# A pooled attention and feed-forward kernel: the fifth tile's scores move into the first run, the first batch's main keys times v become one float32 product, and two later steps move

## The chip, the cores and the metric

The kernel runs on one core of a Trainium2 chip. The metric is the device time of the whole program in microseconds (us), the median of several runs.

TensorE (PE) multiplies, with its weight loads shown apart as PEld. VectorE (DVE), ScalarE (ACT) and GpSimd (POOL) do the elementwise work, and SyncE (SP) issues most of the DMAs. All of them have queues of their own and meet at semaphores.

## The reference

```python
# q, k, v: (8, 8, 576, 64): batch, heads, tokens, head size
k_p = k.reshape(B, H, 72, 8, D).mean(axis=3)
v_p = v.reshape(B, H, 72, 8, D).mean(axis=3)
scores = scale * q @ k_p.T;  scores -= scores.max(-1)
attn = exp(scores);  attn = attn / (attn.sum(-1) + 1e-9)
x = (attn @ v_p) as tokens x 512          # 4608 x 512
h = x @ w_in                              # 512 -> 2048
out = maximum(0.01 * h, h) @ w_out        # 2048 -> 512
```

Everything is float32. Each head has 72 pooled keys; the kernel treats 64 of them as main keys and the last 8 as a remainder.

## The kernel before

The feed-forward part has most of the work. Its products are made of float32r parts: a value is split into a high part (a cast) and a low part (the value less the high part), and three products stand for one (high by high, high by low, low by high). The weights are split in the same way on the chip, by steps that `convert` makes: two ScalarE instructions (L209, L210) and three VectorE instructions (L211, L212, L215) in the first step, a ScalarE cast (L219) and a VectorE subtraction (L220) in the second.

The tokens lie in nine chunks of 512. The first two batches' first 512 tokens are chunks 0 and 1, their last 64 tokens each go into `x_tail`, and the others follow. `runs` lists the passes over the feature tiles: the first run takes chunk 0 with feature tiles 0 to 7, the next two runs take halves of chunk 1 with the same tiles, the fourth and fifth runs take the other eight tiles for chunks 1 and 0, and from the sixth run on a chunk has all sixteen. The seventh run is the fourth chunk (index 3). The last chunks are done with sums of weight blocks, formed earlier by `prepare` (L1192 on VectorE with casts L1195 and subtractions L1199), put into DRAM by POOL's DMA queue (`put_away`, L1179) and read back in the last runs.

In a run, a feature tile has a first product `m1` (ph, L1143 to L1145, twelve instructions), a leaky ReLU and a split (L1148, L1151 on ScalarE, L1152 on VectorE), and two tiles later a second product `m2` (acc, L1361 to L1363). `ph` has two banks. Each half of `m1` and of `m2` is a beat. Attention steps are set between the beats: step i of a run's list goes out when its share of the beats is reached. In the first run that list starts with `TAIL_STEPS`, and the second batch follows.

The steps of a batch are written as names with a tile and a group of four heads: `q` transposes a tile of queries, `sa` makes scores and their exponentials (pss L600, reduction L608, e L610), `sb` divides by the sums (L621, L622 on VectorE, `at` L624 and L628 on POOL), `pu` transposes the attention (pp L701) and splits it (pT, L703, L706, L710), `au` multiplies it with v (pa, L725 to L728, four products for each pair of heads) and splits the result into x (L744, L745). `ku` and `vu` put pooled k and v in place: for v that is `v_hi` (L513), `v_lo` (L516) and the remainder (L522 to L531). `FIRST` is the order of the first batch's steps, in which `c` is a step of the weights; all of it stands ahead of the first run.

TensorE's order is as written (`manual_schedule`). The orders of VectorE, ScalarE, POOL and SP are made by a list scheduler when the program is built: among instructions that it takes to be ready, the one written earlier goes first, and an instruction that is ready runs ahead of its place in the text if its engine is free. From the last runs on POOL and SP are as written, too.

Outputs go from the accumulator into tiles `o` (three buffers), the left half by ScalarE (L1400) and the right half by VectorE (L1401), and then by a DMA to `out`.

```python
PLAN = {REST + 1: (2, 10, 36), REST + 2: (3, 3, 34), REST + 3: (1, 3, 20), REST + 4: (2, 3, 34)}
...
    forming, formed = (sums_in(n), 0) if n in PLAN else (None, 0)
    many, begin, until = PLAN.get(n, (0, 0, 1))
...
    while forming and formed < min(1, (beat - begin) / (until - begin)) * STEPS_OF * many:
```

`REST` is 4, so the entry `REST + 2` is the seventh run: three pairs of weight sums, in seven steps each, from beat 3 until beat 34.

Of the kernel before, what the change touches and what calls it, by code (L numbers as in the profile page):

```python
# [10 lines left out]
F32 = mybir.dt.float32  # L11
F32R = mybir.dt.float32r
# [12 lines left out]
def tile_pooled_attention_ffn(  # L25
# [9 lines left out]
    nc = tc.nc  # L35
# [32 lines left out]
    )  # L68
    TAIL_STEPS = "pu40 au20 pu41 au21"
# [77 lines left out]
    }  # L147

# [17 lines left out]
    def spare(f, i, shape, dtype, name):  # L166

        return wts.tile(shape, dtype, tag=f"w{i}_{f}", name=name)
# [272 lines left out]
    def pin(ins):  # L441
        return tc.keep_in_program_order(ins) if pinned else ins
# [57 lines left out]
    def place_v(b, sums, rem):  # L500
# [10 lines left out]
        for i in range(2):  # L511
            r = slice(64 * i, 64 * i + 64)
            pin(nc.scalar.mul(v_hi[r, :, i, :], sums[r], 1.0 / POOL))  # L513
        for i in range(2):
            r = slice(64 * i, 64 * i + 64)
            pin(nc.vector.scalar_tensor_tensor(  # L516
                v_lo[r, :, i, :], sums[r], 1.0 / POOL, v_hi[r, :, i, :].bitcast(F32),
                op0=ALU.mult, op1=ALU.subtract,
            ))
# [166 lines left out]
    def piece_tiles(b, j, g):  # L686
        if b > 0 or g == 0 or j == 2:
            return pT
        return {
            part: spare(10 - n // 2, n % 2, t.shape, F32R, f"pT_{part}{b}_{j}_{g}")  # L690
            for n, (part, t) in enumerate(pT.items())
        }

    def p_unit(b, t, g, at, pc, o):
# [8 lines left out]
        ins = nc.scalar.copy(pc["hi"][:, :, o : o + n], pp[:, 0:3, :n])  # L703
        if b == 0:
            anchor["act"] = ins
        nc.vector.tensor_tensor(  # L706
            pc["lo"][:, :, o : o + n], pp[:, 0:2, :n], pc["hi"][:, 0:2, o : o + n].bitcast(F32),
            op=ALU.subtract,
        )
# [4 lines left out]
    def av_unit(b, j, g, pc):  # L714
# [3 lines left out]
        for i in range(2):  # L718
# [6 lines left out]
            nc.tensor.matmul(pa, vh, pc["hi"][:, i, :w], start=True, stop=False)  # L725
            nc.tensor.matmul(pa, vh, pc["lo"][:, i, :w], start=False, stop=False)  # L726
            nc.tensor.matmul(pa, vl, pc["hi"][:, i, :w], start=False, stop=False)  # L727
# [760 lines left out]
    for n, pieces in enumerate(beside):  # L1488
# [15 lines left out]
        if n == REST:  # L1504

            us.insert(2, lambda: None)
            units[-1] = [lambda: None] * AHEAD + us[:AHEAD]
            us = us[AHEAD:]
# [12 lines left out]
    PLAN = {REST + 1: (2, 10, 36), REST + 2: (3, 3, 34), REST + 3: (1, 3, 20), REST + 4: (2, 3, 34)}  # L1521
# [152 lines left out]
```

## Time and profile before

| | us |
|---|---|
| median of 3 runs | 916.62 |
| lowest and highest | 916.54 to 917.75 |
| the profiled execution's own time | 916.26 |
| its span | 914.4 |

The span lies from the first to the last recorded instruction; 1.86 us of the profiled execution's time lie around it. In the rows, a time is in us from the start of the span, "x4" is a number of instructions, and a bracket at the end of a row gives how long the engine stood idle ahead of it and what released it. Every float32 product, such as L600, is recorded as two instructions, and a float32r product as one. The engines work in a pipeline, so the length of an instruction is longer than the step to the next one; where a rate is meant, it is the difference of two starts. The clock is a share of full speed: 1.00 is 2.4 GHz and 0.50 is 1.2 GHz.

### The profile page before, as it was taken

Reading aid. Unit: us, or ns where it says so; the run is one execution under the profiler, and the core shown is the slowest. Engines: PE = TensorE matmul, PEld = TensorE weight load, DVE = VectorE, ACT = ScalarE, POOL = GpSimd, SP = SyncE. Lnnn points to the kernel's source line nnn. Section 1 sums busy time; section 2 is a strip of 40 time slices with the busy share of each in tenths; the row PEclk is TensorE's granted clock in tenths of the full one; section 3 lists DMA queues with packets and bytes.
Section 4 is the critical chain, followed back from the end, with each engine's and each line's share of the span. In section 5 each row is a group of like instructions: output and inputs, shape, how many; then the busy total and the mean of one; then the engine's idle time right before and its main releaser. Section 6 shows DMA issues by size and latency. Waiting matters only on the chain.

```text
span 914.4 us, 14169 instructions
## 1 busy us (share of the span) xinstructions
PE 886.6 (97%) x4731; PEld 764.5 (84%) x4731; DVE 520.4 (57%) x1229; ACT 446.2 (49%) x1397; POOL 257.6 (28%) x458
## 2 busy tenths in 40 slices
PE   5689999999999999999999999999999999999998
PEld 4568889887888888888888888888999999999997
DVE  6999569546377654874456437655665643342222
ACT  5798559345244533543454336353654553353322
POOL 4511110342527432552243134624320230010000
PEclk9799999999999999999999999999999999999999
DMA  9965231327356542644254317630875254425332
GB/s 268 315 205 168 63 76 47 84 64 198 98 162 155 137 89 73 184 124 106 51 144 116 103 31 195 162 104 1 204 211 144 67 153 141 124 77 161 104 112 74
DMA packets 151321, 116.53 MB, mean 127 GB/s; under 512 B 100689, under 2 KB 127825, under 8 KB 151249
## 3 DMA queue, kind: packets, MB, share of 16 engines
q1 hardware_dynamic: 136272, 82.47, 34.2%
q10 hardware_dynamic: 11904, 24.78, 9.3%
q0 software_dynamic: 3072, 8.39, 2.6%
q8 instruction: 37, 0.61, 0.3%
q14 instruction: 36, 0.29, 0.1%
HBM read 85.07 MB, written 30.54 MB: 126 GB/s over the span
## 4 chain that ended last, share of the span: by engine, by line
PE 84%; DVE 4%; DMA 3%; ACT 2%; POOL 2%; SPq 1%; issue 1%; POOLq 0%; DVEq 0%; ACTq 0%
PE acc L1361 13%; PE acc L1362 13%; PE acc L1363 13%; PE ph L1143 8%; PE ph L1145 8%; PE ph L1144 8%; PE ends_y L1268 7%; PE ends_x L1268 6%; PE pss L600 3%; PE pa L726 1%; PE pa L728 1%; PE pa L727 1%; PE pa L725 1%; DMA v1raw<-in_v_dram 1%; DVE x_tail L1192 1%
## 5 line engine op out<-in xcount | busy, mean ns | idle before, releaser
L1361 PE MATMUL acc<-w,gh 128*128 128x512 f32 x576 | 227.9, 396 | 1.2 <-DVE o L1401 1.2
L1362 PE MATMUL acc<-w,gh 128*128 128x512 f32 x576 | 225.4, 391 | 0.0
L1363 PE MATMUL acc<-w,gl 128*128 128x512 f32 x576 | 224.6, 390 | 0.0
L1143 PE MATMUL ph<-xh,w 128*128 128x512 f32 (+1 forms) x416 | 159.2, 383 | 1.6 <-DVE gl L1152 1.6
L1144 PE MATMUL ph<-xl,w 128*128 128x512 f32 (+1 forms) x416 | 155.9, 375 | 0.0
L1145 PE MATMUL ph<-xh,w 128*128 128x512 f32 (+1 forms) x416 | 155.9, 375 | 0.0
L1363 PEld LDWEIGHTS acc<-w,gl 128*128 128x128 f32 x576 | 108.1, 188 | 23.9 <-DVE gl L1152 0.5
L1361 PEld LDWEIGHTS acc<-w,gh 128*128 128x128 f32 x576 | 108.6, 188 | 21.0 <-DVE o L1401 1.7
L1362 PEld LDWEIGHTS acc<-w,gh 128*128 128x128 f32 x576 | 108.5, 188 | 18.0
L610 ACT ACTIVATE e<-pss,red 128x72 f32<-128x72 f32 (+1 forms) x320 | 97.6, 329 | 43.6 <-DVE red L608 43.4
L1148 ACT ACTIVATE ph<-ph 128x512 f32<-128x512 f32 (+1 forms) x104 | 58.0, 558 | 87.9 <-PE ph L1145 87.4
L1152 DVE TENSOR_TENSOR gl<-ph,gh 128x512 fp32r<-128x512 f32 (+1 forms) x104 | 66.6, 641 | 54.3 <-ACT gh L1151 53.8
L1143 PEld LDWEIGHTS ph<-xh,w 128*128 128x128 f32 x416 | 78.7, 189 | 15.3 <-DVE gl L1152 2.1
L1145 PEld LDWEIGHTS ph<-xh,w 128*128 128x128 f32 x416 | 78.6, 189 | 14.2
L1144 PEld LDWEIGHTS ph<-xl,w 128*128 128x128 f32 x416 | 78.8, 189 | 12.9
L644 POOL TENSOR_TENSOR at<-e,red 128x128 f32<-128x128 f32 (+1 forms) x120 | 50.6, 442 | 129.6 <-DVE red L641 74.8
L610 ACT ACTIVATION_READ_ACCUMULATOR e<-pss,red 128x1 f32 (+1 forms) x320 | 68.8, 215 | 0.0
L681 DVE STREAM_TRANSPOSE pp<-blocks 128x384 f32<-128x384 f32 (+1 forms) x60 | 44.5, 760 | 39.7 <-DMA blocks<-rows 39.5
L608 DVE TENSOR_REDUCE red<-pss 128x4 f32<-128x288 f32 (+1 forms) x80 | 35.8, 452 | 52.4 <-PE pss L600 51.1
L703 ACT CAST pT_hi<-pp 128x384 fp32r<-128x384 f32 (+1 forms) x80 | 36.9, 479 | 49.7 <-DVE pp L681 46.0
L1151 ACT CAST gh<-ph 128x512 fp32r<-128x512 f32 (+1 forms) x104 | 57.9, 556 | 2.5
L600 PEld LDWEIGHTS pss<-kT,qT 128*128 128x128 f32 x320 | 47.0, 199 | 6.4 <-ACT qT L577 1.5
(293 smaller groups left out, 1529.1 us busy)
## 6 DMA issues: line engine op xcount, KB each, us to landing
seat<-kept ACTq DMA_DIRECT2D x31, 512.0 KB
rows<-at SPq DMA_DIRECT2D x48, 192.0 KB
blocks<-rows SPq DMA_DIRECT2D x48, 192.0 KB
out_dram<-o SPq DMA_DIRECT2D x34, 256.0 KB
w_bits<-in_moe_w_in_dram SPq DMA_DIRECT2D x16, 512.0 KB
w_bits<-in_moe_w_out_dram SPq DMA_DIRECT2D x16, 512.0 KB
q<-in_q_dram SPq DMA_DIRECT2D x96, 64.0 KB
w<-kept ACTq DMA_DIRECT2D x21, 256.0 KB
```

What stands on the lines that cost most here:

```text
L600: nc.tensor.matmul(sc[:, 2 * SP * i : 2 * SP * (i + 1)], qT[:, p, :], kT[:, p, :, :].rearrange("d i s -> d (i s)"), start=True, stop=True,)
L610: ins = nc.scalar.activation(e[:n, h, :], scv[:n, h, :], AF.Exp, bias=mx[:n, h : h + 1], accum_out=sm[:n, h : h + 1],)
L1143: nc.tensor.matmul(ph, w[:, 0, ks], xh[kk][:, r], start=kk == 0, stop=False)
L1144: nc.tensor.matmul(ph, w[:, 0, ks], xl[kk][:, r], start=False, stop=False)
L1145: nc.tensor.matmul(ph, w[:, 1, ks], xh[kk][:, r], start=False, stop=kk == NK - 1)
L1148: nc.scalar.activation(ph, ph, AF.Prelu, alpha=0.01)
L1151: casts.append(nc.scalar.copy(gh, ph))
L1152: lows.append(nc.vector.tensor_tensor(gl, ph, gh.bitcast(F32), op=ALU.subtract))
L1268: nc.tensor.matmul(out, w[:, stay, ks], move, start=start and i + n == 0, stop=i + n == 3, skip_group_check=True,)
L1361: nc.tensor.matmul(a, gh[:, r], hi, start=first, stop=False)
L1362: nc.tensor.matmul(a, gh[:, r], lo, start=False, stop=False)
L1363: nc.tensor.matmul(a, gl[:, r], hi, start=False, stop=last)
```

## The change

The scores of the first batch's fifth tile (`sa40 sa41 sb40 sb41`) leave `FIRST` and become the first four steps of the first run's list. For the first batch, the product of the 64 main keys with v is a single float32 product of whole values (`v_whole`, `whole`), where there were three float32r products; so the low parts of attention and of v are not formed, and the ScalarE copy of the transposed attention becomes two, one for the remainder and one for the main keys. The remainder's product stays. The third batch's `vu` (index 2, `att[VIA]`) is written some steps later, behind `sb11`. The weight sums of the fourth chunk's run are formed from beat 8 until 37. `v_whole` lies in the buffer that later holds a part of the second chunk's x, and so do the `whole` tiles.

```diff
--- before.py
+++ after.py
@@ -64,9 +64,9 @@
     FIRST = (
         "lk ku q0 q1 sa00 sb00 sa01 sb01 lv sa10 sb10 sa11 sb11 q2 sa20 sa21 vu pu00 pu10 c c q3 "
         "pu01 pu11 c sb20 sb21 au00 sa30 sa31 c au01 c pu20 pu21 sb30 sb31 c c pu30 pu31 c au10 au11 "
-        "c q4 c c / sa40 sa41 sb40 sb41 c c c"
+        "c q4 c c / c c c"
     )
-    TAIL_STEPS = "pu40 au20 pu41 au21"
+    TAIL_STEPS = "sa40 sa41 sb40 sb41 pu40 au20 pu41 au21"
     VIA = 2
     SPLIT = 8
     HALF = CH // 2
@@ -145,6 +145,9 @@
         "hi": const.tile([P, 3, PMAX], F32R, name="pT_hi"),
         "lo": const.tile([P, 2, PMAX], F32R, name="pT_lo"),
     }
+
+    v_whole = one.tile([P, NK, 2, D], F32, tag="xl1_1", name="v_whole")
+    nc.gpsimd.memset(v_whole, 0.0)
 
     tiny = const.tile([P, 4], F32, name="tiny")
     nc.gpsimd.memset(tiny, 1e-9)
@@ -510,8 +513,11 @@
             sums = pvm.rearrange("a (p d) -> a p d", p=NK)
         for i in range(2):
             r = slice(64 * i, 64 * i + 64)
-            pin(nc.scalar.mul(v_hi[r, :, i, :], sums[r], 1.0 / POOL))
-        for i in range(2):
+            if b == 0:
+                nc.scalar.mul(v_whole[r, :, i, :], sums[r], 1.0 / POOL)
+            else:
+                pin(nc.scalar.mul(v_hi[r, :, i, :], sums[r], 1.0 / POOL))
+        for i in range(2 if b else 0):
             r = slice(64 * i, 64 * i + 64)
             pin(nc.vector.scalar_tensor_tensor(
                 v_lo[r, :, i, :], sums[r], 1.0 / POOL, v_hi[r, :, i, :].bitcast(F32),
@@ -684,12 +690,13 @@
         return pp
 
     def piece_tiles(b, j, g):
-        if b > 0 or g == 0 or j == 2:
+        if b > 0:
             return pT
-        return {
-            part: spare(10 - n // 2, n % 2, t.shape, F32R, f"pT_{part}{b}_{j}_{g}")
-            for n, (part, t) in enumerate(pT.items())
-        }
+        hi = pT["hi"]
+        if g and j < 2:
+            hi = spare(10, 0, hi.shape, F32R, f"pT_hi{b}_{j}_{g}")
+        whole = one.tile([P, 2, CH // 2], F32, tag=f"xl1_{2 + g}", name=f"pT_whole{b}_{j}_{g}")
+        return {"hi": hi, "whole": whole}
 
     def p_unit(b, t, g, at, pc, o):
         n = tiles[b][t][1]
@@ -700,13 +707,16 @@
             for i in range(3):
                 nc.tensor.transpose(pp[:, i, :n], at[:n, i, :], ident[:n, :n])
         rem = pc["hi"][:, 2, o : o + n]
-        ins = nc.scalar.copy(pc["hi"][:, :, o : o + n], pp[:, 0:3, :n])
         if b == 0:
-            anchor["act"] = ins
-        nc.vector.tensor_tensor(
-            pc["lo"][:, :, o : o + n], pp[:, 0:2, :n], pc["hi"][:, 0:2, o : o + n].bitcast(F32),
-            op=ALU.subtract,
-        )
+
+            nc.scalar.copy(rem, pp[:, 2, :n])
+            anchor["act"] = nc.scalar.copy(pc["whole"][:, :, o : o + n], pp[:, 0:2, :n])
+        else:
+            nc.scalar.copy(pc["hi"][:, :, o : o + n], pp[:, 0:3, :n])
+            nc.vector.tensor_tensor(
+                pc["lo"][:, :, o : o + n], pp[:, 0:2, :n],
+                pc["hi"][:, 0:2, o : o + n].bitcast(F32), op=ALU.subtract,
+            )
         nc.vector.scalar_tensor_tensor(
             rem, pp[:, 2, :n], m_lo, rem.bitcast(F32), op0=ALU.mult, op1=ALU.subtract
         )
@@ -722,9 +732,13 @@
             vh = v_hi[:, p, :, :].rearrange("a i d -> a (i d)")
             vl = v_lo[:, p, :, :].rearrange("a i d -> a (i d)")
             vr = v_rem[:, g, 2 * i : 2 * i + 2, :].rearrange("a i d -> a (i d)")
-            nc.tensor.matmul(pa, vh, pc["hi"][:, i, :w], start=True, stop=False)
-            nc.tensor.matmul(pa, vh, pc["lo"][:, i, :w], start=False, stop=False)
-            nc.tensor.matmul(pa, vl, pc["hi"][:, i, :w], start=False, stop=False)
+            if b == 0:
+                vw = v_whole[:, p, :, :].rearrange("a i d -> a (i d)")
+                nc.tensor.matmul(pa, vw, pc["whole"][:, i, :w], start=True, stop=False)
+            else:
+                nc.tensor.matmul(pa, vh, pc["hi"][:, i, :w], start=True, stop=False)
+                nc.tensor.matmul(pa, vh, pc["lo"][:, i, :w], start=False, stop=False)
+                nc.tensor.matmul(pa, vl, pc["hi"][:, i, :w], start=False, stop=False)
             nc.tensor.matmul(pa, vr, pc["hi"][:, 2, :w], start=False, stop=True)
             if b < 2:
                 c, o, m = b, s0, max(0, min(n, CH - s0))
@@ -1504,6 +1518,8 @@
         if n == REST:
 
             us.insert(2, lambda: None)
+            us.remove(att[VIA]["vu"])
+            us.insert(us.index(att[VIA]["sb11"]) + 1, att[VIA]["vu"])
             units[-1] = [lambda: None] * AHEAD + us[:AHEAD]
             us = us[AHEAD:]
         units.append(us)
@@ -1518,7 +1534,7 @@
     for b, n in loads_at.items():
         early[max(n, REST) - 1].append(b)
 
-    PLAN = {REST + 1: (2, 10, 36), REST + 2: (3, 3, 34), REST + 3: (1, 3, 20), REST + 4: (2, 3, 34)}
+    PLAN = {REST + 1: (2, 10, 36), REST + 2: (3, 8, 37), REST + 3: (1, 3, 20), REST + 4: (2, 3, 34)}
     STEPS_OF = 7
     left = list(range(len(PAIRS)))
 
```

## Rows read from the trace of the kernel before

**Rows 1.** The page: busy time, share and instructions of each engine.

```profile
PE 886.6 (97%) x4731; PEld 764.5 (84%) x4731; DVE 520.4 (57%) x1229; ACT 446.2 (49%) x1397; POOL 257.6 (28%) x458
```

**Rows 2.** Windows: busy us (x instructions) of PE, PEld, DVE, ACT, POOL; clock; DMA.

```profile
24.50:45.27 20.77, 12.97 (x64) 10.91 (x64) 20.62 (x50) 15.30 (x47) 12.04 (x17) 0.75 1.02 311
45.27:64.14 18.87, 16.56 (x82) 12.67 (x80) 17.98 (x42) 18.19 (x48) 2.60 (x4) 0.91 0.58 185
64.14:92.13 27.99, 27.99 (x147) 23.38 (x145) 26.78 (x57) 22.39 (x67) 3.99 (x6) 1.00 0.60 187
```

**Rows 3.** Waits of TensorE, whole execution: us, times, longest.

```profile
PE pp L701 <- POOL at L624: 7.7, 3, 5.0
...
PE pss L600 <- DVE xl L745: 1.7, 2, 1.0
```

**Rows 4.** Timeline of TensorE before the first run: start, length.

```profile
25.61 0.41 PE L728 MATMUL pa<-pT_hi,v_rem 128*128 128x256 f32 x1
25.83 2.12 PE L600 MATMUL pss<-kT,qT 128*128 128x144 f32 x8
27.73 0.55 PE L725 MATMUL pa<-pT_hi,v_hi 128*128 128x256 f32 x1
...
35.11 0.90 PE L701 MATMUL pp<-ident,at 128*128 128x128 f32 x3 [5.01 <-POOL at L624]
...
37.48 0.56 PE L725 MATMUL pa<-pT_hi,v_hi 128*128 128x256 f32 x1
...
41.85 0.47 PE L572 MATMUL pq<-ident,q 64*128 64x64 f32 x4
...
45.27 0.80 PE L1143 MATMUL ph<-xh,w 128*128 128x512 f32 x1
```

**Rows 5.** Windows around the first run's start, columns as before.

```profile
38.40:41.80 3.40, 3.34 (x14) 2.92 (x13) 3.38 (x8) 3.40 (x9) 1.50 (x3) 0.50 1.01 351
41.80:45.27 3.47, 1.75 (x14) 1.38 (x13) 3.38 (x10) 1.69 (x6) 0.00 (x0) 0.99 1.03 358
45.27:48.60 3.33, 3.33 (x11) 2.65 (x10) 2.80 (x9) 2.65 (x17) 0.36 (x1) 0.50 0.89 347
```

**Rows 6.** Groups by line and form, 12 to 50 us: busy, mean ns.

```profile
L703 ACT CAST pT_hi<-pp 128x384 fp32r<-128x384 f32 x8 | 3.7, 488 | 0.1
...
L706 DVE TENSOR_TENSOR pT_lo<-pp,pT_hi 128x256 fp32r<-128x256 f32 x8 | 3.3, 414 | 0.0
...
L516 DVE SCALAR_TENSOR_TENSOR v_lo<-pvm,v_hi 64x256 fp32r<-64x256 f32 x2 | 0.8, 406 | 0.0
```

**Rows 7.** Timeline of TensorE in the first run.

```profile
53.21 0.30 PE L726 MATMUL pa<-pT_lo,v_hi 128*128 128x64 f32 x1 [0.82 <-DVE pT_lo L706]
...
57.91 0.19 PE L725 MATMUL pa<-pT_hi,v_hi 128*128 128x64 f32 x1
...
58.83 0.48 PE L1143 MATMUL ph<-xh,w 128*128 128x512 f32 x1
```

**Rows 8.** Timeline of ScalarE, 40 to 43 us.

```profile
41.75 0.53 ACT L538 ACTIVATE v_parts<-vremsum 32x64 fp32r<-32x64 f32 x2
```

**Rows 9.** Timeline of ScalarE around the third batch's v.

```profile
199.23 0.31 ACT L522 ACTIVATE v_parts<-vremsum 128x128 fp32r<-128x128 f32 x1 [5.29 <-POOL vremsum L272]
199.45 0.57 ACT L1151 CAST gh<-ph 128x512 fp32r<-128x512 f32 x1
```

**Rows 10.** Timeline of TensorE at the fifth run's start.

```profile
207.25 0.50 PE L1143 MATMUL ph<-xh,w 128*128 128x512 f32 x1 [1.11 <-DVE gl L1152]
```

**Rows 11.** Timeline of VectorE at the seventh run's start.

```profile
360.59 1.07 DVE L1401 COPY o<-acc 128x256 f32<-128x256 f32 x3
```

**Rows 12.** Timeline of ScalarE there.

```profile
365.67 0.37 ACT L1400 COPY o<-acc 128x256 f32<-128x256 f32 x1 [2.08 <-DMA out_dram<-o]
```

**Rows 13.** Timeline of TensorE there.

```profile
359.17 0.39 PE L1363 MATMUL acc<-w,gl 128*128 128x512 f32 x1
...
366.55 0.50 PE L1361 MATMUL acc<-w,gh 128*128 128x512 f32 x1 [1.24 <-DVE o L1401]
```

## The prediction

> **What bounds the kernel now.** I read the page's shares first. TensorE is busy 886.6 of 914.4 us [rows 1], so all of its idle time together is 27.8 us, and a change can only win by taking some of that away or by shortening TensorE's own work. The windows say where it lies. From 24.5 to 45.27 us TensorE works 12.97 of 20.77 us, from 45.27 to 64.14 us 16.56 of 18.87, and from 64.14 to 92.13 us it is full. In the same three windows VectorE is busy 20.62, 17.98 and 26.78 us, and ScalarE 18.19 of the 18.87 us in the second [rows 2]. So the stretch ahead of the first run and its first third are set by VectorE, with ScalarE close behind; all later stretches by TensorE.
>
> The table of TensorE's waits names the parts: 7.7 us on POOL's division of the attention, 1.7 us of scores on xl [rows 3]. The timeline puts them in order. TensorE stands 5.01 us until 35.11, starts the second piece's product with v at 37.48 and the fifth tile's query transposes at 41.85, and then its scores wait for xl twice. The first run starts at 45.27 [rows 4]. Everything behind it is TensorE work in a fixed order, so that start moves the end one for one as long as the other engines keep up.
>
> The clock matters here too. From 38.4 to 41.8 us TensorE is busy 3.34 of 3.40 us at half clock; in the next stretch, the one with the two waits, it has full clock but works 1.75 of 3.47 us; and the first products of the run then have half clock again [rows 5].
>
> **The fifth tile's scores move.** Ahead of the first run there now stand only the two products of the second piece (four pairs of heads) and the transposes. Their price changes as well, by the float32 product. A float32 product of 144 columns at half clock: from 25.83 to 27.73 us go eight instructions, which are four products, so 0.475 us each and 3.3 ns a column; a float32r product of 256 columns takes 25.83 less 25.61, 0.22 us [rows 4]. No row has a float32 product of 256 columns, so I scale by columns: 0.845 us at half clock, and with the remainder's 0.22 a pair costs 1.065 us. Four pairs: 4.26 us from 37.48, so 41.74; before, they took 4.37 us until 41.85, for three of the cheaper products and the waits between them. The price goes up by 0.19 us a pair and the waits for low parts go away: about even. Bounds: if a whole product cost only as much as the three (0.66), it would be 0.7 us earlier; if the waits stayed, about 0.7 us later. With the transposes' 0.47 us the first run starts at 42.2 us in place of 45.27: 3.1 us.
>
> The Trainium skill's page "FP8 and Floating Point Precision", section "TensorE Precision Notes", says that a true float32 product takes four passes through the array. By that rule the whole product is four passes in place of three, which speaks against this part of the change; it would be 0.85 us a pair here, the same as by the row, so the sum stands by either.
>
> The half clock of the first products follows a stretch with two waits; without these the run's products fill that stretch. At half clock 3.33 us of work costs 1.67 us too much [rows 5], which I count as won. (Below: nothing, if the fall comes anyhow.)
>
> Inside the run TensorE now has the scores: four products at full clock, 0.24 us each by halving 0.475, a cost of 0.95 us. The fifth tile's product with v gets shorter. Eight products of 64 columns take 58.83 less 57.91, 0.92 us, so 0.115 each [rows 7]; a float32 product of 64 columns is 0.11 by the rate above, so three become one and four pairs save eight times 0.115, 0.92 us. The two cancel. Of the wait of 0.82 us for the low part [rows 7] I take half, 0.4 us: the low part is gone, but the remainder still comes by ScalarE and then VectorE (both ends: 0 and 0.82).
>
> TensorE could thus be 3.1 + 1.67 − 0.95 + 0.92 + 0.4 = 5.1 us earlier.
>
> **The cover for that.** VectorE has to be as much earlier, as it makes the weights' parts and gl for the run and has been full from 24.5 us on. What it is relieved of: eight subtractions for the low part of attention, 3.3 us, and two for that of v, 0.8 us [rows 6]; 4.1 us. The reductions and divisions of the fifth tile stay its work, only later. ScalarE gets eight more copies; the row has 488 ns for the copy of 384 columns that is now split [rows 6], so the extra is between 0 and eight times that, 3.9 us; since the columns don't grow I take a third, 1.3 us. It had idle time ahead of the run to hold that (15.30 busy of 20.77) and none in the run's first third [rows 2]. I therefore let the smaller number count: 4.1 us, and the other 1.0 us comes back as waits in the first run. POOL gets one memset at its start; it is busy 12.04 of 20.77 us, and its work for the division stands behind the second batch's sums, so I leave its times where they are, though the exponentials should be ready sooner (a gain that I don't count).
>
> **The third batch's v.** ScalarE's instruction for the remainder of v (L522) waited 5.29 us for POOL, and the cast gh of a feature tile stood behind it [rows 9]; that lateness runs on through VectorE's gl to TensorE's wait of 1.11 us at 207.25 [rows 10]. Writing `vu` later would take that away if ScalarE's queue followed the text. It doesn't. The second batch's v remainder belongs to the first run's beat 13, some 17 us behind 45.27 (13 half products of six times 0.22), and ran at 41.75 [rows 8], ahead of the run. The scheduler puts such an instruction where it believes the input to be ready and the engine free; its place in the text is only the second key, and `lv`, which makes the input, hasn't moved. I take 0; the bounds are a gain of 1.11 us and, if it now stands in front of something more urgent, a loss of the same size.
>
> **The fourth chunk's sums.** Here the text does bind, as each step is queued behind the latest gl that has been written. In the old order the first sums stand among the previous run's outputs. The last product of that run starts at 359.17 [rows 13], VectorE copies its three halves from 360.59 [rows 11], the DMA of the first buffer is late by as much, ScalarE's fourth copy waits 2.08 us for it [rows 12], and TensorE stands 1.24 us until 366.55 [rows 13]. Beat 8 is the end of exactly that product (two halves of `m2`, two of `m1`, two, and two), so the sums now follow the copies. With the copies some 1.4 us sooner (at the last product's end) the wait of 1.24 us goes. Bounds: 0 and 1.24. The sums end three beats later, about 4 us, with 27 beats left: nothing waits for them there. POOL's DMA issues move with them and stand in its queue between the divisions for the next chunk, as they did.
>
> **The sum.** 916.26 us is the profiled execution's own time, 1.86 us of it outside the span. Less 4.1 and 1.24 it is 910.9. The median of the runs is 0.36 us higher, so 911.3 us.
>
> **The rivals.**
> - *Also v.* The queue does change and the 1.11 us go: 910.2. Rows 9 and 10 show that there is something to win, row 8 that the place in the text hardly decides.
> - *Taken back by ScalarE and VectorE.* ScalarE is full from 45 to 64 us; the extra copies and a start 3 us earlier bring more waits, or the weights' steps float up into VectorE's free time. If only a third of the 4.1 us stays, 1.4: 916.62 − 1.4 − 1.24 = 914.0. If nothing stays, 915.4, within what the measurement can't tell from no change (0.2%, 1.8 us).
> - *The wait at the outputs moves.* The fourth output still waits for a buffer: 912.5.
> - *Slower: the fifth tile's transposes in the run.* TensorE takes its steps in order. Between `sa40` (beat 1) and `pu40` (beat 5) stand 24 products of 512 columns; at full clock each takes what 256 columns took at half, 0.22 us [rows 4], together 5.3 us. The fourth tile's chain from its scores at 25.83 to its transposes at 35.11 [rows 4] took 9.3 us. As long a chain means a wait of 4.0 us, and by what rows 5 show a fall of the clock behind it, 1.7 us: 5.7 us, which eats the gain of 5.3. From about 9 us up the change is slower; with a chain of 12 us it would be 916.6 − 5.3 + 6.7 + 1.7 = 919.7. Against it: before the run both engines were shared with the other tiles, which are done by then.
>
> **How the numbers follow.** The forecast has 0.40, also v 0.18, taken back in part 0.16, the moved wait 0.06, no change in sum 0.11, slower 0.09. So faster by over 0.2% is 0.80, the same 0.11, slower 0.09. The forecast alone spans 909.9 (the uncounted gain of POOL's earlier division, some 1 us, and the wait at 53.21) to 912.6 (clock not won). The range for 8 in 10 goes from 908.8, where v pays as well, to 915.2, the near end of no change; the slower case and most of "the same" are left out.
>
> **What would show it.** Right: the first ph product near 42 us with the granted clock at 1.00 in the stretch behind it; no L706 before the second batch and VectorE still full until about 60 us; TensorE full from about 60 us; no wait at L1361 near 362; L522 still ahead of gh near 195 us with a wait of some microseconds. Wrong: the first ph product at 44 us or later, a wait of more than 3 us at L701 in the first run, a half clock past 50 us, or a new wait where the sums now lie, from 359 to 400 us.

## The result: the changed kernel is slower

The changed kernel takes 923.02 us (921.24 to 924.70, 6 runs) against 917.12 us (916.54 to 918.29, 6 runs) for the kernel before on the same chip: a ratio of 1.0061, with a 95% interval of 1.0048 to 1.0075. The forecast was 911.3 us, in a range up to 915.2. The profiled execution is the longest of the six, 924.70 us with a span of 922.9, so its rows show 8.5 us of difference where the medians differ by 5.9. The lines of the kernel after stand 3 to 14 further down: L212 is the L209 of before, L616 its L610, L758 its L744, L1157 its L1143 and L1166 its L1152.

The page's busy times of the kernel after, beside [rows 1]: TensorE works 4.7 us longer, though its instructions are 12 fewer.

```profile
PE 891.3 (97%) x4719; PEld 765.0 (83%) x4719; DVE 516.7 (56%) x1217; ACT 447.3 (48%) x1407; POOL 258.3 (28%) x459
```

The windows of the kernel after, from the same start, and as long behind the first run's start as those of [rows 2]:

```profile
24.50:41.80 17.30, 9.44 (x40) 6.81 (x39) 16.99 (x37) 15.69 (x51) 12.23 (x17) 0.80 1.00 297
41.80:60.67 18.87, 14.51 (x54) 10.82 (x55) 16.77 (x37) 14.27 (x43) 3.08 (x5) 0.82 0.74 249
60.67:88.66 27.99, 25.82 (x117) 20.66 (x117) 21.23 (x46) 17.50 (x47) 2.13 (x4) 0.88 0.47 149
```

The first run starts at 41.80, 3.47 us sooner. In its first 18.87 us TensorE then does 2 us less than before and at a clock of 0.82; and ScalarE, which was full there [rows 2], is idle for 4.6 us. In the next 28 us, which were full, TensorE still stands for 2.2 us and the clock is 0.88. The first run (from its first ph to the next run's) in a row for each kernel, before and then after:

```profile
45.27:104.76 59.49, 57.18 (x293) 46.73 (x291) 50.41 (x111) 46.13 (x130) 8.54 (x14) 0.97 0.50 156
```

```profile
41.80:112.69 70.89, 63.72 (x294) 50.89 (x294) 51.41 (x113) 46.28 (x135) 8.58 (x15) 0.90 0.47 150
```

It is 11.40 us longer: TensorE's idle time went from 2.31 to 7.17 us (4.86 more) and its busy time up by 6.54. The clock accounts for most of the latter, by an estimate: 70.89 us at a mean of 0.90 lack 7.1 us of full clock, 59.49 us at 0.97 lack 1.8, so at most 5.3 us, as a part of either stretch is idle time; the scores are the rest. Later the fifth run is shorter by 0.73 us (49.17 for 49.90) and the seventh longer by 0.86 (97.37 for 96.51); the others differ by 0.4 us in all. So 11.40 − 3.47 − 0.73 + 0.86 + 0.4 = 8.5 us: **the loss lies in the first run alone.**

TensorE's timeline in that run, the waits (the last row answers to [rows 10]):

```profile
41.80 0.50 PE L1157 MATMUL ph<-xh,w 128*128 128x512 f32 x1 [1.13 <-ACT xh L758]
43.96 0.79 PE L1158 MATMUL ph<-xl,w 128*128 128x512 f32 x1 [1.66 <-DVE xl L759]
...
53.97 0.80 PE L1157 MATMUL ph<-xh,w 128*128 128x512 f32 x1 [1.98 <-DVE red L627]
...
60.02 0.30 PE L742 MATMUL pa<-pT_hi,v_rem 128*128 128x64 f32 x1 [0.72 <-DVE pT_hi L720]
...
65.00 0.43 PE L737 MATMUL pa<-pT_whole,v_whole 128*128 128x64 f32 x2 [0.94 <-ACT pT_whole L713]
...
214.86 0.50 PE L1157 MATMUL ph<-xh,w 128*128 128x512 f32 x1 [0.41 <-DVE gl L1166]
```

The wait at 41.80 comes from ScalarE, and that at 43.96 begins there. ScalarE's queue in the kernel after reads:

```profile
36.42 0.68 ACT L212 ACTIVATE w_bits<-w_bits 128x512 f32<-128x512 f32 x1
...
40.35 0.67 ACT L213 ACTIVATE w_bits<-w_bits 128x512 int32<-128x512 uint32 x1
40.90 0.58 ACT L222 CAST w<-w_t 128x512 fp32r<-128x512 f32 x1
41.37 0.92 ACT L758 CAST xh<-pa 128x256 fp32r<-128x256 f32 x3
...
49.51 0.32 ACT L616 ACTIVATE e<-pss,red 64x72 f32<-64x72 f32 x1 [3.69 <-DVE red L614]
...
50.71 0.58 ACT L1162 ACTIVATE ph<-ph 128x512 f32<-128x512 f32 x1
...
52.60 0.59 ACT L1165 CAST gh<-ph 128x512 fp32r<-128x512 f32 x1
```

Four conversion heads (a head is the first step of a conversion, on ScalarE two instructions; here eight from 36.42 on) now run ahead of the casts of the second piece's x. In the program a head is queued behind the latest attention instruction of the first batch on ScalarE (`anchor["act"]`) until three casts exist; with the scores gone from `FIRST`, that is a copy at 36.16 and no longer the fifth tile's exponentials. Then ScalarE stands for 3.69 us, as its next instruction is an exponential that waits for a reduction; the leaky ReLU of the first feature tile, whose products end near 48.7, stands behind it until 50.71, and gh behind the other four exponentials. VectorE shows the other ends of this: xl waits behind a conversion step too, the reduction comes late, behind three more from 47.22 on, and gl follows gh.

```profile
42.90 0.68 DVE L223 TENSOR_TENSOR w<-w_t,w 128x512 fp32r<-128x512 f32 x1
43.50 1.07 DVE L759 TENSOR_TENSOR xl<-pa,xh 128x256 fp32r<-128x256 f32 x3
...
47.22 1.29 DVE L223 TENSOR_TENSOR w<-w_t,w 128x512 fp32r<-128x512 f32 x2
48.44 0.69 DVE L215 SCALAR_TENSOR_TENSOR w_t<-w_bits,w_t 128x512 int32<-128x512 int32 x1
49.03 0.44 DVE L614 TENSOR_REDUCE red<-pss 64x4 f32<-64x288 f32 x1
...
53.22 0.69 DVE L1166 TENSOR_TENSOR gl<-ph,gh 128x512 fp32r<-128x512 f32 x1 [0.68 <-ACT gh L1165]
```

gl ends at 53.91, just ahead of 53.97, where TensorE needs that feature tile's bank; the row names red L627, which only ends at the same time. This is the largest of the waits.

### The profile page after: what moved, and what is told of

Same layout as the page of the kernel before. It is cut to its first block, busy times and chain, and to the rows that moved or that the text cites. A ratio compares the mean times of both kernels' runs of the same rounds, so it can differ in the third digit from the quotient of the medians.

```text
span 922.9 us, 14159 instructions
## 1 busy us (share of the span) xinstructions
PE 891.3 (97%) x4719; PEld 765.0 (83%) x4719; DVE 516.7 (56%) x1217; ACT 447.3 (48%) x1407; POOL 258.3 (28%) x459
## 4 chain that ended last, share of the span: by engine, by line
PE 85%; DVE 7%; ACT 3%; DMA 2%; issue 1%; POOL 1%; SPq 0%; DVEq 0%; POOLq 0%; ACTq 0%
PE acc L1375 13%; PE acc L1376 13%; PE acc L1377 13%; PE ph L1159 8%; PE ph L1157 8%; PE ph L1158 8%; PE ends_y L1282 7%; PE ends_x L1282 6%; PE pss L606 4%; ACT e L616 2%; DMA blocks<-rows 1%; DVE x_tail L1206 1%; PE pa L742 1%; PE pa L740 1%; PE pa L741 1%
## 5 line engine op out<-in xcount | busy, mean ns | idle before, releaser
L1157 PE MATMUL ph<-xh,w 128*128 128x512 f32 (+1 forms) x416 | 159.9, 384 | 4.3 <-DVE red L627 2.0
L616 ACT ACTIVATE e<-pss,red 128x72 f32<-128x72 f32 (+1 forms) x320 | 97.9, 330 | 45.6 <-DVE red L614 44.5
L1166 DVE TENSOR_TENSOR gl<-ph,gh 128x512 fp32r<-128x512 f32 (+1 forms) x104 | 66.7, 641 | 55.7 <-ACT gh L1165 55.3
L1157 PEld LDWEIGHTS ph<-xh,w 128*128 128x128 f32 x416 | 79.1, 190 | 19.5 <-DVE gl L1166 2.4
L616 ACT ACTIVATION_READ_ACCUMULATOR e<-pss,red 128x1 f32 (+1 forms) x320 | 68.9, 215 | 0.0
L715 ACT CAST pT_hi<-pp 128x384 fp32r<-128x384 f32 (+1 forms) x70 | 32.5, 482 | 51.2 <-DVE pp L687 47.3
```

The lines of the kernel that those rows point to most:

```text
L616: ins = nc.scalar.activation(e[:n, h, :], scv[:n, h, :], AF.Exp, bias=mx[:n, h : h + 1], accum_out=sm[:n, h : h + 1],)
L1157: nc.tensor.matmul(ph, w[:, 0, ks], xh[kk][:, r], start=kk == 0, stop=False)
L1166: lows.append(nc.vector.tensor_tensor(gl, ph, gh.bitcast(F32), op=ALU.subtract))
```

## The experiments

Four theories of the loss: conversion heads run ahead of urgent work (A, the anchor); the float32 product is dear (B); the fifth tile's steps follow too closely on each other in the run (C); ScalarE and VectorE are full there (D). In each title stand the median and the ratio to the kernel before, with its interval; "first run" is its start, length, and TensorE's idle time in it, from the one profiled execution, which can lie some us from the median.

**The score move alone, on the kernel before.** 921.27 us, 1.0054 (1.0038 to 1.0071). First run 43.37, 68.21, 6.33.

```diff
-        "c q4 c c / sa40 sa41 sb40 sb41 c c c"
+        "c q4 c c / c c c"
-    TAIL_STEPS = "pu40 au20 pu41 au21"
+    TAIL_STEPS = "sa40 sa41 sb40 sb41 pu40 au20 pu41 au21"
```

> The kernel before with one part of the change: the fifth tile's scores and divisions are the first steps of the first run. Theory A (the weights' conversions are tied behind the latest attention step on ScalarE; without the fifth tile's exponentials ahead of the run they start some 5 us too early and stand in front of the casts of x and of the first product's ReLU): slower than before by 4 to 10 us, 921 to 927, with the first ph product waiting for xl and ScalarE's conversions L209/L210 in a block ahead of L744. Theory B (the float32 product and the two copies in place of one are the cost): within 2 us of before or faster, 912 to 919. Theory C (TensorE waits for the fifth tile's own chain inside the run, whatever the conversions do): slower by 4 to 10 us, with the waits at L701 and L725 of the fifth tile, not at xl or gl.

**The float32 product alone.** 916.49 us, 1.0003 (0.9994 to 1.0013). First run 43.14, 59.75, 3.07. The edit is the part of the diff with `v_whole` and `whole`, without the other three.

> The kernel before with one part of the change: the first batch's main keys times v as one float32 product. Theory A: faster by 1 to 4 us, 913 to 916, as VectorE is relieved of 4.1 us and the fifth tile's exponentials still hold the conversions back. Theory B: slower by 4 to 10 us, 921 to 927. Theory C: as theory A.

**All of the change but the score move.** 915.61 us, 0.9998 (0.9983 to 1.0014). First run 43.31, 59.73, 4.34, at a clock of 1.00. The edit is the reverse of the diff above.

> The changed kernel with the fifth tile's scores put back ahead of the first run. Theory A and C: the loss in the first run goes; with v's step (the gain of 0.7 us in the fifth run of the profile) and the sums (a loss of 0.9 us in the seventh) about 913 to 917. Theory B: stays at 921 to 925.

These three place the loss. The score move alone makes 4.9 us of it, and without the move nothing is lost. B falls: with the product the first run starts 2.0 to 2.1 us sooner and is as long as before. There the lead does reach the run's end (102.89 us with the product alone, for 104.76), but not the program's: in that profile two later waits grow, from 1.2 us at the outputs and 0.2 us at a low part of attention to these.

```profile
PE acc L1375 <- DVE o L1415: 1.8, 1, 1.8
PE pa L740 <- DVE pT_lo L716: 1.2, 1, 1.2
```

With the score move alone, TensorE's largest wait in the first run is not for gl but for a cast of the weights:

```profile
57.31 0.75 PE L1143 MATMUL ph<-xh,w 128*128 128x512 f32 x1 [3.51 <-ACT w L219]
```

**The changed kernel, with the casts of x as an anchor too.** 920.14 us, 1.0041 (1.0026 to 1.0056). First run 40.66, 67.72, 9.16.

```diff
-                nc.scalar.copy(h, pa[:, :m])
+                ins = nc.scalar.copy(h, pa[:, :m])
+                if b == 0:
+                    anchor["act"] = ins
```

> The changed kernel with one more tie: the cast of the first batch's x (the ScalarE copy after the product with v) also becomes the instruction behind which the next conversions are queued; nothing else is moved. Theory A: the wait of the first run's second product for xl (1.66 us in the profile of the changed kernel) goes, the first run gets at least 4 us shorter than its 70.9 us, and the time falls to 914 to 919. Theory C: no more than 1.5 us won, 921 or above, as the waits for the fifth tile's chain stay. Theory B: as C.

**The kernel before, its fifth tile's exponentials no longer an anchor.** 917.70 us, 1.0013 (1.0004 to 1.0023). First run 49.01, 57.62, 1.24.

```diff
-        if b == 0:
+        if b == 0 and t < 4:
             anchor["act"] = ins
```

> The kernel before, but the fifth tile's exponentials no longer count as the latest attention instruction behind which ScalarE's conversion heads are queued; the scores stay where they were. Theory A (the score move lets conversion heads run ahead of the second piece's casts, and that is what costs): three heads of 1.1 us each run ahead of the fifth tile's exponentials here too, so the first run loses 2 to 4 us, 918.5 to 920. Theories C and D (the fifth tile's chain inside the run, or ScalarE and VectorE being full there) don't touch this kernel: 915.5 to 917.5.

A holds for a part. With the anchor, the waits for xh and xl are gone, and so is most of the half clock (0.97); by the ratios some 1.8 us of 5.6, with intervals that overlap. In the second kernel the same heads make TensorE wait for xl in its scores,

```profile
47.12 2.26 PE L600 MATMUL pss<-kT,qT 128*128 128x144 f32 x8 [4.66 <-DVE xl L745]
```

but 3.74 us of later start become 1.87 us at the first run's end and 1.2 us in the time. **The start of the run alone does not set its end.** The kernel with the anchor shows what does: it starts soonest of these, and TensorE stands again for the first feature tile's gl (the wait of 2.62 us; L1168 is here the L1152 of before), and then for the fifth tile's copies and remainders. Its gh is done near 48.6, and gl then stands behind conversion steps on VectorE.

```profile
50.73 0.80 PE L1159 MATMUL ph<-xh,w 128*128 128x512 f32 x1 [2.62 <-DVE gl L1168]
...
57.20 0.44 PE L737 MATMUL pa<-pT_whole,v_whole 128*128 128x64 f32 x2 [1.53 <-ACT pT_whole L713]
58.70 0.30 PE L742 MATMUL pa<-pT_hi,v_rem 128*128 128x64 f32 x1 [1.07 <-DVE pT_hi L720]
...
64.04 0.30 PE L742 MATMUL pa<-pT_hi,v_rem 128*128 128x64 f32 x1 [1.16 <-DVE pT_hi L720]
```

```profile
48.14 1.27 DVE L223 TENSOR_TENSOR w<-w_t,w 128x512 fp32r<-128x512 f32 x2
49.34 0.68 DVE L218 CUSTOM_DVE_ANT_0 w_t<-w_bits,w_t 128x1024 uint16<-128x1024 uint16 x1
...
50.03 0.65 DVE L1168 TENSOR_TENSOR gl<-ph,gh 128x512 fp32r<-128x512 f32 x1
```

The next kernels with the score move are this one with one or two more edits each; those without the move don't have the added anchor. In the edits "-" is an empty step.

**Fifth tile two steps later.** 924.84 us, 1.0084 (1.0060 to 1.0108). First run 39.84, 71.33, 9.81.

```diff
-            us = [att[0][u] for u in TAIL_STEPS.split()] + us
+            names = "- - sa40 sa41 sb40 sb41 pu40 au20 pu41 au21".split()
+            us = [us.pop(0) if u == "+" else att[0][u] if u != "-" else (lambda: None) for u in names] + us
```

> The changed kernel with the xh anchor (920.1), its fifth tile's scores and all that follows set two steps later in the first run. Theory C (each hop of the fifth tile's chain is too close to the next in TensorE's order): the chain keeps its spacing, the waits of 1.5, 1.1 and 1.2 us at its products with v stay, 919.5 to 920.5. Theory D (ScalarE and VectorE are full in the first third of the run, so anything that comes less densely there helps): the first two Prelu instructions are no longer behind the exponentials, the wait of 2.6 us for gl and its 1.7 us of half clock go, 916 to 917.5.

Both theories miss. The run starts 0.8 us sooner still, and TensorE stands longer for the same gl, which comes at the same time (50.14 for 50.03): what TensorE wins ahead of it is given back whole. The run ends 2.8 us later than with the anchor alone; another wait of 1.64 us lies far from it, at 691.20.

```profile
50.87 0.79 PE L1159 MATMUL ph<-xh,w 128*128 128x512 f32 x1 [4.28 <-DVE gl L1168]
```

```profile
50.14 0.68 DVE L1168 TENSOR_TENSOR gl<-ph,gh 128x512 fp32r<-128x512 f32 x1
```

**Conversions asked for later.** 918.66 us, 1.0022 (1.0011 to 1.0033). First run 39.89, 65.79, 7.41; its profiled execution is its shortest, 916.21 us.

```diff
-                convert_to(14 + 2.8 * f)
+                convert_to(8 + 3.6 * f)
```

> The changed kernel with the xh anchor (920.1), the weights' conversions of the first run asked for later: step 8 + 3.6 f in place of 14 + 2.8 f, so up to three or four steps fewer stand in the queues from 44 to 60 us, with nothing left out. Theory D: ScalarE and VectorE get some 3 us freer there, the waits for gl and for the attention fall by 2 to 4 us, 916 to 918. Theory C: the chain's own length is the cost, 919.5 to 920.5. If the weights come too late, a wait on w takes it back: above 920.5.

**Room between the fifth tile's steps.** 919.77 us, 1.0032 (1.0019 to 1.0045). First run 41.07, 66.11, 6.93.

```diff
-            us = [att[0][u] for u in TAIL_STEPS.split()] + us
+            names = "sa40 sa41 sb40 sb41 - pu40 - au20 pu41 - au21".split()
+            us = [us.pop(0) if u == "+" else att[0][u] if u != "-" else (lambda: None) for u in names] + us
```

> The changed kernel with the xh anchor (920.1), with one empty step ahead of the fifth tile's transposes and one between each transposition and its product with v. Theory C: the waits of 1.5, 1.1 and 1.2 us there go, 916 to 917. Theory D: what is late is ScalarE's and VectorE's whole work, so the time comes back as waits on gl or w: 919 to 920.5.

These two speak for D, if not by much: less in the queues is worth 1.7 us by the ratios, with intervals that overlap and a time between the two expectations. Room is worth 0.8 us, which the intervals don't tell from nothing; in its profile, the longest of its executions, the waits at the products with v are shorter (0.60 and 0.51 us for the first two), and the time comes back elsewhere, 1.0 us of it on the weights.

**Part of the conversion left out, on both engines; on VectorE alone; on both, without the score move.** 916.08 us, 1.0002 (0.9990 to 1.0013), first run 41.15, 64.42, 5.86; 918.44 us, 1.0020 (1.0011 to 1.0029), first run 40.09, 65.33, 6.46; 913.48 us, 0.9966 (0.9954 to 0.9978), first run 43.11, 58.89, 2.16.

```diff
-                nc.scalar.activation(low, low.bitcast(U32), AF.Copy, scale=2.0**-29)
+                if f not in (3, 4, 5):
+                    nc.scalar.activation(low, low.bitcast(U32), AF.Copy, scale=2.0**-29)
...
-            nc.vector.tensor_tensor(t, t, low, op=ALU.add)
+            if f not in (3, 4, 5):
+                nc.vector.tensor_tensor(t, t, low, op=ALU.add)
```

> The changed kernel with the xh anchor (920.1), with part of the weights' conversion left out: for the feature tiles 3 to 5 the low word of the weights is neither scaled on ScalarE nor added on VectorE (six instructions of some 0.56 us on ScalarE and six of 0.60 us on VectorE less, which fall between 42 and 62 us), so those weights lose their last bits. Theory D (ScalarE and VectorE are full in the first third of the run and set the time): the 3.4 us come back nearly whole, 916 to 917.5. Theory C (the hops of the fifth tile's chain): its waits of 1.5, 1.1 and 1.2 us stay, 919 to 920.5.

> The same, but only VectorE's six additions of the low word are left out; ScalarE still scales it. If VectorE is the full engine of theory D, the time is that of the kernel without both, 916 to 917.5; if ScalarE is, hardly anything comes back, 919 to 920.5.

> The changed kernel with the fifth tile's scores put back ahead of the run (915.6), with the same part of the conversion left out on both engines. Theory D: ScalarE and VectorE bind less here, the waits of the first run sum to some 3 us, of which those on gl and the attention (2.5 us) can go at most; a gain of 0 to 2 us, 913.5 to 915.6, smaller than in the kernel with the scores inside the run. Theory C says nothing of it: the same gain in both kernels.

Six instructions on each engine, 3.4 and 3.6 us, bring back 3.6 us by the ratios (1.0041 to 1.0002), about half of it by VectorE alone. That is D: in this stretch work on these two engines is time. But without the score move the same omission brings 2.9 us, so D holds there as well and hardly explains the distance between the two kernels, which goes from 3.9 to 3.3 us.

**The same omission, with room.** 916.06 us, 1.0008 (0.9991 to 1.0025). First run 39.39, 63.41, 5.87, at a clock of 1.00; its profiled execution, 913.74 us, is its second shortest.

> The changed kernel with the xh anchor and the part of the conversion left out for the feature tiles 3 to 5 (916.1), and in addition an empty step ahead of the fifth tile's transposes and one between each transposition and its product with v. If, with ScalarE and VectorE relieved, the chain's hops are what is left of the loss (theory C): the waits of 1.2 and 1.5 us there go, 913.5 to 915. If not: 915.5 to 917.

**The fifth tile's exponentials left out; the same without the score move.** 917.12 us, 1.0011 (0.9997 to 1.0025); 913.27 us, 0.9955 (0.9939 to 0.9971).

```diff
+        if b == 0 and t == 4:
+            nc.vector.tensor_reduce(out=sm[:n], in_=scv[:n], axis=AX.X, op=ALU.max)
+            ins = nc.scalar.copy(e[:n], scv[:n])
+        else:
...
```

The lines under `else` are the old reduction and the four exponentials.

> The changed kernel with the xh anchor (920.1), with the fifth tile's eight exponentials left out: ScalarE makes one plain copy of each group's scores, which doesn't wait for the reduction, and the sums are the maxima. ScalarE has some 1.7 us less, and nothing of the first run is queued behind a reduction. If the exponentials' place in ScalarE's queue is the rest of the loss: the wait of 2.6 us for gl and its half clock go, 916 to 917. If only their 1.7 us of work counts: 918.5 to 919.5.

> The same in the changed kernel with the scores put back ahead of the run (915.6). If the exponentials cost by their place in the run only: 914.5 to 915.6 here, a gain much smaller than in the other kernel. If by their work: the same gain of 1 to 1.7 us in both, 914 to 914.6.

C falls as far as these edits test it, and so does the exponentials' place in ScalarE's queue: with the omission, room changes nothing, and without the exponentials the kernel with the move gains 2.7 us and the one without it 3.9. The distance between the kernels with and without the move stays at 3 to 5 us under the omission and without the exponentials. In the pair with part of the conversion left out it reads, from these two windows (with the move, and without), as TensorE's idle time, 3.70 us more, and busy time, 1.83 us more at the same clock, less 1.96 us of earlier start. The first of these two executions lies 2.4 us above its median.

```profile
41.15:105.57 64.42, 58.56 (x295) 47.19 (x294) 47.68 (x107) 45.27 (x133) 9.21 (x17) 0.97 0.54 172
```

```profile
43.11:102.00 58.89, 56.73 (x289) 46.16 (x287) 45.17 (x101) 43.40 (x126) 7.95 (x14) 0.97 0.53 171
```

Part of the idle time is late in the run: in that kernel with the move, TensorE waits 1.3 us for an exponential of the second batch and 0.6 us at one of its products with v, and without the move at neither. The list of the first run is four steps longer for the same beats, so the second batch's steps follow later and more closely. That this is the rest was not tried.

**The third batch's v alone.** 914.91 us, 0.9985 (0.9976 to 0.9993): faster by 0.15%.

```diff
+            us.remove(att[VIA]["vu"])
+            us.insert(us.index(att[VIA]["sb11"]) + 1, att[VIA]["vu"])
```

> The kernel before with the later place of the third batch's v alone. By the prediction (queues don't follow the text): no change, 916 to 917, the wait ahead of the fifth run's products at 207 us stays. By the rival that it pays: 1.1 us less, 915.4.

The fifth run is 1.44 us shorter and has no wait. VectorE's timeline shows one reason, first of the kernel before, then of this one:

```profile
201.08 0.69 DVE L531 TENSOR_TENSOR v_rem<-vremsum,heads 128x512 fp32r<-128x512 f32 x1
201.69 0.81 DVE L608 TENSOR_REDUCE red<-pss 128x4 f32<-128x288 f32 x2
```

```profile
199.42 0.81 DVE L608 TENSOR_REDUCE red<-pss 128x4 f32<-128x288 f32 x2
...
201.08 0.67 DVE L531 TENSOR_TENSOR v_rem<-vremsum,heads 128x512 fp32r<-128x512 f32 x1
```

The remainder's last step stood ahead of a reduction for which eight exponentials waited, with casts and the leaky ReLU behind them; now it stands behind. In the changed kernel it does too. The other reason is a load that the edit doesn't move: in this profile the input of the remainder landed sooner, as POOL's rows show (the kernel before, then this one).

```profile
196.57 2.09 POOL L265 TENSOR_TENSOR vremraw<-vremraw 128x512 f32<-128x512 f32 x2 [2.13 <-DMA vremraw<-in_v_dram]
```

```profile
195.01 2.10 POOL L265 TENSOR_TENSOR vremraw<-vremraw 128x512 f32<-128x512 f32 x2 [1.14 <-DMA vremraw<-in_v_dram]
```

Each is worth about 0.7 us in these profiles. The score move alone has the old order, and POOL stands there for 1.14 us too; the changed kernel has the new order, and POOL waits 2.40 us for the load. Both have a fifth run of 49.17 us, 0.73 less than before.

**The fourth chunk's sums alone.** 916.44 us, 1.0003 (0.9993 to 1.0012).

```diff
-    PLAN = {REST + 1: (2, 10, 36), REST + 2: (3, 3, 34), REST + 3: (1, 3, 20), REST + 4: (2, 3, 34)}
+    PLAN = {REST + 1: (2, 10, 36), REST + 2: (3, 8, 37), REST + 3: (1, 3, 20), REST + 4: (2, 3, 34)}
```

> The kernel before with the fourth chunk's sums from beat 8 alone. By the prediction: the wait of 1.24 us at the outputs goes, 915.3. By the rival that the wait moves (new waits between 359 and 420 us): no change or slower, 916.3 to 917.5.

The wait at the outputs [rows 13] is gone, and two new ones stand behind the sums, of 1.64 us together:

```profile
395.49 0.49 PE L1143 MATMUL ph<-xh,w 128*128 128x512 f32 x1 [1.03 <-DVE gl L1152]
407.39 0.76 PE L600 MATMUL pss<-kT,qT 128*128 128x144 f32 x4 [0.61 <-DVE xl L745]
```

**The product and the later v, and these with the later conversions.** 916.03 us, 0.9999 (0.9989 to 1.0010); 915.83 us, 1.0000 (0.9991 to 1.0009).

> The kernel before with the float32 product and the later v alone (scores ahead of the run, sums where they were). If the two add up as measured one by one (no change and 1.5 us): 914 to 915.5, faster than before. If the float32 product's earlier start is worth something here: below 914.

> The same with the weights' conversions of the first run asked for at step 8 + 3.6 f in place of 14 + 2.8 f. Theory D: 1 to 2 us less than without, 912.5 to 914.5, as ScalarE and VectorE are freer for the first products' gl. If the scores' place is what made them the limit: no change, 914 to 915.5.

The gain of v is not seen again beside the float32 product (0.4 us between 1.0003 and 0.9999, with intervals that overlap), though in the first one's profile, the longest of its executions, the fifth run is 0.68 us shorter (49.22); there the wait at the outputs of the seventh run is 2.6 us in place of 1.24. The later conversions bring nothing without the score move, and 1.7 us with it. So they lower the distance between the kernels with and without the move to 2.0 us (1.0022 and 1.0000; these two differ in the added anchor and in the sums too, and the sums alone are worth 0.0003): the crowd of conversions behind the earlier start is a part of what the move costs. Of the kernels that do the whole work, only the one with v alone is faster than the kernel before.

## Why the prediction was wrong

- **The first run's start** came out near the forecast, 41.80 us for 42.2, and in part by luck: the products began at 35.75 in place of 37.48, as POOL's division ended sooner, and TensorE then stood for 1.13 us for xh, which the sum doesn't have. The price is right: the pair of products at half clock, put at 1.065 us by scaling, takes 1.06 to 1.08 (below, from one start of L737 to the next). But the start was taken to move the end one for one. With the scores in the run that is not so: the 3.47 us of lead of the changed kernel and 0.8 more in the kernel with the later fifth tile were lost within the run, and of the 3.74 us less in the one without the anchor half was made up. The product alone kept 1.87 us to the run's end, and lost most of it later.

```profile
35.75 1.06 PE L737 MATMUL pa<-pT_whole,v_whole 128*128 128x256 f32 x2
...
36.83 1.05 PE L737 MATMUL pa<-pT_whole,v_whole 128*128 128x256 f32 x2
```

- **The cover** is the step that failed. It counted VectorE's relief of 4.1 us as time that the run keeps, ScalarE's extra as hidden, and at worst 1.0 us of new waits. The run had 4.86 us of new waits, ScalarE 3.69 us of standing in its own order at the worst moment, and the score move alone cost 4.9 us. The prediction put at nothing, without a reason, what moves on the two engines when the scores leave: the heads that had been queued behind them run ahead (some 1.8 us by the kernel with the anchor), and the conversions crowd the run's first part (some 1.7 us by the later conversions). The two together, 1.0061 to 1.0022, are clear of the intervals.
- **The rival "taken back"** named this, with the weights' steps that float up, but its worst case was that nothing of the lead stays, 915.4; the helpers took back more than the lead (923.02).
- **The half clock** was counted as a gain of 1.67 us. The clock fell again behind the waits for xl and gl, and for longest, from 67.5 to 74 us (0.52 and 0.50 in two windows there), behind the waits at the products with v; it cost up to 5.3 us more than before. The forecast's 912.6 for a clock that isn't won doesn't come out of its terms either: 3.4 us of lead in place of 4.1 give 912.0.
- **The scores in the run** were put at 0.95 us; TensorE's busy time rises by 1.8 to 1.9 us at equal clock.
- **The fifth tile's product with v** and its wait: 0.82 us of wait was to be halved; it became 0.72 us for a remainder, 0.94 for a copy and 0.52 for the second remainder.
- **v** was put at nothing, as `L522` would stay ahead of gh. It does (a wait of 5.58 us in the changed kernel), but the lateness came by VectorE's `v_rem` ahead of a reduction, which does follow the text. The rival "also v" was right for v alone, with 1.4 us; in the fifth run's profile about half of it is the place in the text, and half the sooner load.
- **The sums** were put at 1.24 us. That wait went, and 1.64 us came back as waits for gl and xl, 30 to 40 us later (in the changed kernel 0.75 and 0.67 us of the same kinds, at 396.61, 402.83 and 414.81): 27 beats were left, but VectorE's queue had no room in them.
- **The rival on the slower side** had the sign, and a price near it (919.7), but not the place: TensorE doesn't wait for the fifth tile's transposes (they start at 56.83, behind the wait for gl). It waits for what stands behind that tile's work in ScalarE's and VectorE's queues.

Of the signs named, the first ph near 42 us, no low part of attention before the second batch, no wait at the outputs and the remainder of v ahead of gh came true. The full clock behind the start, VectorE full until 60 us (16.77 of 18.87) and TensorE full from 60 us did not, and two of the four signs against it, half clock past 50 us and new waits near the sums, are there.

What stays open: the 2.0 us between the kernels with and without the score move that the anchor and the later conversions leave, and which neither room nor the exponentials explain; why the omission, though it frees the same engines, hardly lowers the distance; and why v's gain is lost beside the float32 product.

## What to carry to other kernels

When two helper engines are full behind the start of a stretch, an earlier start of the bottleneck engine is worth only what their next deliveries allow: find the first of these (here gl, which starts at 49.3 to 50.4 us in the kernels with the anchor and the whole conversion, whatever TensorE did) and count the gain up to it. A step that is moved also takes away what the scheduler hung on it, so look for orders, such as an anchor, that refer to "the latest" instruction. Before a wait is counted as won, name the queue that gets the moved work and what stands behind it there.

## What was unexpected of the hardware

Idle time and clock don't go together simply: the changed kernel lost its clock in the first run (0.90 with 7.17 us of idle time), the kernel with part of the conversion left out and room kept 1.00 with 5.87 us, and the one with the anchor had 0.97 with 9.16 us. The Trainium skill's page "TensorE: Matmul & The Clock Gate", section "Part 1: The HAM clock gate", says that half rate is the default which recent activity releases. The trace agrees: in the changed kernel half clock follows the waits at 65.00 us and just behind (0.50 from 71 to 74 us), and full clock follows once TensorE has been full from 67.5 us on (1.00 from 78 to 83); the rows here don't show which of the waits decides.

The executions of some of these kernels spread by 0.8 to 0.9% (the change without the score move: 913.2 to 920.4 us; the omission with room: 912.8 to 920.8), those of the kernel before by 0.5% (914.8 to 919.1 us in 35), which no single profile shows. What makes the difference was not tried.
